# Decay masks of six attention heads: from a DRAM scratch read back by SyncE, to six transfers out of SBUF rows issued by ScalarE

## The chip, the cores and the metric

The kernel runs on one core of a Trainium2 chip. The metric is the device time of one launch, in microseconds. The profile names the engines PE (TensorE; PEld is its weight loads), DVE (VectorE), ACT (ScalarE), POOL (GpSimd) and SP (SyncE). SPq and ACTq are the moments at which SyncE and ScalarE issue a DMA.

## What is computed

Three blocks follow each other: a linear attention with decay, a token-mixing and channel-mixing MLP, and a Fourier mixing with a second MLP. The change lies in the attention, whose reference is:

```python
rel = pos[:, None] - pos[None, :]
Dmask = np.where(rel >= 0, lam[:, None, None] ** rel[None, :, :], 0.0)
for b in range(nb):
    intra = np.einsum('bhic,bhjc->bhij', qb, kb) * Dmask[None]
    intra = np.einsum('bhij,bhjd->bhid', intra, vb)
    inter = np.einsum('bhid,bhde->bhie', qb * lam_pow[None], kv_state)
    out[:, :, sl] = intra + inter
    kv_state = lam_block[None, :, None, None] * kv_state + np.einsum('bhsd,bhse->bhde', kb_dec, vb)
```

There are 2 batches, 8 heads, 768 positions and 64 channels a head, all in float32. Each head has its own decay `lam[h]`, and so its own mask: a triangle of powers of `lam[h]`.

## The kernel before

Heads are taken two at a time: a pair fills the 128 partitions, and there are four pairs in each of two batches. I call them pairs 0 to 3 (first batch) and 4 to 7 (second). The kernel uses blocks of 128 positions, six a sequence. For each pair SyncE loads `kp` (k transposed, 384 KB, L377), q (384 KB, L372) and k with v (768 KB, L373).

`attention_setup` (L299) makes the masks. `pw8` has one row a head: 127 zeros, a one, and the powers of that head's `lam`, doubled seven times on DVE (L317). The mask of a head on 128 partitions is that row read at 128 shifted starts, so that partition p holds elements p to p+127. Heads 0 and 1 are built on DVE by another way (L333 to L350). For heads 2 to 7 the rows go to a DRAM scratch of 8 KB (L320), and `skew` (L324) reads them back as overlapping windows: heads 2 to 5 in one transfer of 256 KB, and heads 6 and 7 in one of 128 KB. All of these are issued by SyncE, among the loads of the pairs. The masks lie in `dT`, a part of the tile `att`.

Each pair then runs three steps. `attention_scores` (L381) multiplies q by k on PE (L393), applies the mask on DVE (L396), and scales q on POOL (L400). `attention_states` (L405) scales k on ACT by a column of the mask (L413), forms the block states on PE (L418) and sums them on DVE (L422, L424). `attention_out` (L428) copies the states on ACT (L435), multiplies on PE (L441, L444) and copies the result on ACT (L446). The words of `EARLY` order these steps: s, u and r with the number of the pair, and `x00` for the first transposes of the MLP (`px`, L461).

In the same stretch the first MLP weights arrive as 64-bit words and are converted to float32: a load (`raw_t`, L190; three of 512 KB come first, one for each tile `w_t1`), an ACT pass (`m_t`, L210), three DVE passes (L235, L236, L238), and a split on ACT (L264) and POOL (L265).

The orders of SP and PE are written out by hand: they are the order of the program. A scheduler orders ACT, DVE and POOL. Every engine takes its own instructions strictly in that order. Each DMA is given one of eight completion counters (DMAHW0 to DMAHW7 in the order below). A DMA that gets a counter that is still in use waits, on the engine that issues it, for the transfer that had it before.

Of the kernel before, what the change touches and what calls it, by code (L numbers as in the profile page):

```python
# [25 lines left out]
P = 128  # L26
C = 128
# [34 lines left out]
def body(ctx: ExitStack, tc: tile.TileContext, qkv, kT, lam, w_tok1, w_tok2,  # L62
         w_ch1, w_ch2, m_ch1, m_ch2, dft, dft_x, out, scratch, singles):
    nc = tc.nc
# [41 lines left out]
    def big_tile(n, dt=F32):  # L106
        return big_p.tile([P, BIG], dt, tag="big", name=n)

    def half_tile(shape, n, dt=F32):
        return half_p.tile(shape, dt, tag="half", name=n)  # L110

    def temp(w, n, dt=F32):
        return t_p.tile([P, 2 * NQ + 2], dt, tag="t", name=n)[:, :w]
# [185 lines left out]
    def attention_setup():  # L299

        pw8 = temp(2 * C, "pw8")[:H]
        nc.sync.dma_start(pw8[:, C:C + 1], lam.rearrange("(h o) -> h o", o=1))
        lam_bc = sm_p.tile([P, H], F32, name="lam_bc")
        nc.scalar.dma_start(lam_bc, lam.rearrange("(o h) -> o h", o=1).broadcast_to([P, H]))
        kp = big_tile("kp").rearrange("p (i s) -> p i s", i=4)[:, :, :S]
        kps = [kp[:, i, :].rearrange("p (c j) -> p c j", j=C) for i in range(4)]
        load_kp(0, 0, kps[0])
        t = half_tile([P, 4, S], "qkv_0_0")
        for i in range(3):
            nc.sync.dma_start(t[:, i, :], qkv[0, 0, :, i])  # L310
        load_kp(0, 1, kps[1])
        nc.vector.memset(pw8[:, 0:C - 1], 0.0)
        nc.vector.memset(pw8[:, C - 1:C], 1.0)
        n = 1
        while n < C:
            w = min(n, C - n)
            ts(out=pw8[:, C + n:C + n + w], in0=pw8[:, C:C + w], scalar1=pw8[:, C + n - 1:C + n], scalar2=None,  # L317
               op0=ALU.mult)
            n *= 2
        nc.sync.dma_start(scratch, pw8)  # L320
        att = big_tile("att")
        dT = att[:, 0:H * C].rearrange("p (h j) -> p h j", h=H)

        def skew(h0, h1):  # L324
            src = bass.AP(scratch.tensor, scratch.offset + h0 * 2 * C, [[1, P], [2 * C, h1 - h0], [1, C]])
            nc.sync.dma_start(dT[:, h0:h1, :], src)

        load_qkv(0, 1)
        skew(2, 6)

        bands = [temp(2 * (C // 2 + C), f"band_{i}").rearrange("p (h j) -> p h j", h=2) for i in range(2)]
        for t_ in bands:
            nc.vector.memset(t_[:, :, 0:C // 2], 0.0)  # L333
        for h in range(2):
            nc.vector.tensor_copy(bands[0][:, h, C // 2:], ident[:, ::-1])
        bd = att[:, (H + NP) * C:(H + NP) * C + 2 * (NC - 1) * P]
        cleared = nc.gpsimd.memset(bd, 0.0).ins
        lp = sm_p.tile([P, 7, 2], F32, name="lp")
        n, i = 1, 0
        while n < C:  # L340
            if n == 1:
                by = lam_bc
            else:
                by = lp[:, i]
                was = lam_bc[:, 0:2] if n == 2 else lp[:, i - 1]
                with tc.issue_after(cleared):
                    nc.gpsimd.tensor_tensor(out=by, in0=was, in1=was, op=ALU.mult)
            for h in range(2):
                src = bands[i % 2][:, h]
                built = stt(out=dT[:, h, :] if 2 * n == C else bands[1 - i % 2][:, h, C // 2:],  # L350
                            in0=src[:, C // 2 - n:C // 2 - n + C], scalar=by[:, h:h + 1], in1=src[:, C // 2:],
                            op0=ALU.mult, op1=ALU.add).ins
            n *= 2
            i += 1
        pw = att[:, H * C:(H + NP) * C].rearrange("p (h j) -> p h j", h=NP)
        bd = bd.rearrange("p (i c j) -> p i c j", i=2, c=NC - 1)

        with tc.issue_after(built):
            for a in range(2):
                nc.vector.tensor_copy(pw[a * D:(a + 1) * D, :, 0:1],  # L360
                                      lam_bc[a * D:(a + 1) * D, a::2].rearrange("p (h o) -> p h o", o=1))
        n = 1
        while n < C:
            nc.gpsimd.tensor_tensor(out=pw[:, :, n:2 * n], in0=pw[:, :, 0:n],
                                    in1=pw[:, :, n - 1:n].to_broadcast([P, NP, n]), op=ALU.mult)
            n *= 2
        pair[0, 0] = t
        return dT, pw, kps, [bd[:, i] for i in range(2)], skew

    def load_qkv(b, hp):  # L370
        t = half_tile([P, 4, S], f"qkv_{b}_{hp}")
        nc.sync.dma_start(t[:, 0, :], qkv[b, hp, :, 0])  # L372
        nc.sync.dma_start(t[:, 1:3, :], qkv[b, hp, :, 1:3])  # L373
        pair[b, hp] = t

    def load_kp(b, hp, kp):
        nc.sync.dma_start(kp, kT[b, hp].rearrange("p (c j) -> p c j", j=C))  # L377
# [74 lines left out]
    h1 = {}  # L452
# [527 lines left out]

    with tc.manual_schedule(engines={ENG.SP, ENG.PE}):
        dT, pw, kps, bds, skew = attention_setup()

        def load(n):
# [174 lines left out]
```

## Time and profile before

| | |
|---|---|
| median of 3 runs | 616.99 us (616.93 to 618.64) |
| the profiled execution | 619.19 us, of which its span is 617.2 us |
| PE busy | 592.4 us (96% of the span) |
| DVE, ACT, POOL busy | 411.1, 269.3, 142.0 us |
| mean granted TensorE clock | 0.994 |

The profile's page cuts the span in 40 slices; a digit is the busy share of a slice in tenths. The windows view gives busy times for any stretch. The timeline lists instructions with what ended the idle time before them: `[2.77 <-DMA raw_t_0d<-w_tok]` says that the engine sat idle for 2.77 us until that transfer had landed.

### The profile page before, as it was taken

Reading aid. Unit: us, or ns where it says so; the run is one execution under the profiler, and the core shown is the slowest. Engines: PE = TensorE matmul, PEld = TensorE weight load, DVE = VectorE, ACT = ScalarE, POOL = GpSimd, SP = SyncE. Lnnn points to the kernel's source line nnn. Section 1 sums busy time; section 2 is a strip of 40 time slices with the busy share of each in tenths; the row PEclk is TensorE's granted clock in tenths of the full one; section 3 lists DMA queues with packets and bytes.
Section 4 is the critical chain, followed back from the end, with each engine's and each line's share of the span. In section 5 each row is a group of like instructions: output and inputs, shape, how many; then the busy total and the mean of one; then the engine's idle time right before and its main releaser. Section 6 shows DMA issues by size and latency. Waiting matters only on the chain. (4 is left out here: it accounts for less than half of the span.)

```text
span 617.2 us, 9594 instructions
## 1 busy us (share of the span) xinstructions
PE 592.4 (96%) x3704; PEld 548.0 (89%) x3704; DVE 411.1 (67%) x768; ACT 269.3 (44%) x536; POOL 142.0 (23%) x119
## 2 busy tenths in 40 slices
PE   8699999999999999999999999999899999999997
PEld 7687899899989998999989999879788887888896
DVE  6697896792656336639696876795697677343435
ACT  2566884653555335244453451333543553211110
POOL 5253333220400220111363210034402232300000
PEclk9899999999999999999999999999999999999999
DMA  7964434333378167100132000002404432000005
GB/s 280 404 240 168 165 134 145 103 115 108 102 255 279 50 192 234 49 1 1 53 88 81 21 1 35 18 1 85 132 5 156 134 121 86 1 1 0 1 1 204
DMA packets 24637, 65.58 MB, mean 106 GB/s; under 512 B 2824, under 2 KB 3984, under 8 KB 24592
## 3 DMA queue, kind: packets, MB, share of 16 engines
q1 hardware_dynamic: 24304, 64.83, 31.4%
q8 instruction: 29, 0.48, 0.4%
q10 hardware_dynamic: 288, 0.14, 0.1%
q14 instruction: 16, 0.13, 0.1%
HBM read 54.99 MB, written 9.97 MB: 105 GB/s over the span
## 5 line engine op out<-in xcount | busy, mean ns | idle before, releaser
L499 DVE SCALAR_TENSOR_TENSOR hid<-ph,hid 128x384 fp32r<-128x384 f32 x68 | 37.7, 554 | 59.3 <-ACT hid L498 59.1
L124 PE MATMUL ac<-w_b,hid 128*128 128x512 f32 x192 | 75.9, 396 | 0.3 <-DVE hid L499 0.3
L123 PE MATMUL ac<-w_b,hid 128*128 128x512 f32 x192 | 75.7, 394 | 0.0
L122 PE MATMUL ac<-w_b,hid 128*128 128x512 f32 x192 | 74.9, 390 | 0.0
L498 ACT ACTIVATE hid<-ph 128x384 fp32r<-128x384 f32 x68 | 33.0, 486 | 80.1 <-PE ph L124 80.1
L122 PE MATMUL ac<-hid,w_b 128*128 128x384 f32 x192 | 65.1, 339 | 1.8 <-ACT hid L498 1.8
L123 PE MATMUL ac<-hid,w_b 128*128 128x384 f32 x192 | 64.9, 338 | 1.3 <-DVE hid L499 1.1
L122 PE MATMUL ph<-uh,w_a 128*128 128x384 f32 x192 | 64.7, 337 | 0.4 <-DVE hid L499 0.4
L124 PE MATMUL ph<-uh,w_a 128*128 128x384 f32 x192 | 64.3, 335 | 0.0
L124 PE MATMUL ac<-hid,w_b 128*128 128x384 f32 x192 | 64.2, 334 | 0.0
L123 PE MATMUL ph<-uh,w_a 128*128 128x384 f32 x192 | 64.2, 334 | 0.0
L265 POOL TENSOR_TENSOR w_a<-m_a,w_a 128x512 fp32r<-128x512 f32 x18 | 25.9, 1437 | 98.1 <-ACT w_a L264 79.9
L124 PEld LDWEIGHTS ac<-w_b,hid 128*128 128x128 f32 x192 | 36.0, 188 | 8.4 <-DVE hid L499 0.8
L123 PEld LDWEIGHTS ac<-w_b,hid 128*128 128x128 f32 x192 | 36.0, 188 | 6.1
L122 PEld LDWEIGHTS ac<-w_b,hid 128*128 128x128 f32 x192 | 36.1, 188 | 5.8
L122 PEld LDWEIGHTS ac<-hid,w_b 128*128 128x128 f32 x192 | 36.1, 188 | 3.4 <-ACT hid L498 3.1
L123 PEld LDWEIGHTS ac<-hid,w_b 128*128 128x128 f32 x192 | 36.1, 188 | 3.0 <-DVE hid L499 2.9
L265 POOL TENSOR_TENSOR w_b<-m_b,w_b 128x512 fp32r<-128x512 f32 x18 | 24.5, 1363 | 61.4 <-ACT w_b L264 37.2
L122 PEld LDWEIGHTS ph<-uh,w_a 128*128 128x128 f32 x192 | 36.1, 188 | 0.9 <-DVE hid L499 0.6
L123 PEld LDWEIGHTS ph<-uh,w_a 128*128 128x128 f32 x192 | 36.1, 188 | 0.1
L124 PEld LDWEIGHTS ph<-uh,w_a 128*128 128x128 f32 x192 | 36.0, 188 | 0.0
L124 PEld LDWEIGHTS ac<-hid,w_b 128*128 128x128 f32 x192 | 36.0, 188 | 0.0
(504 smaller groups left out, 1484.1 us busy)
## 6 DMA issues: line engine op xcount, KB each, us to landing
qkv<-qkv SPq DMA_DIRECT2D x7, 768.0 KB, 7.7
single_scratch<-m_a SPq DMA_DIRECT2D x16, 256.0 KB, 5.0
qkv<-qkv SPq DMA_DIRECT2D x10, 384.0 KB, 5.9
kp<-kT SPq DMA_DIRECT2D x8, 384.0 KB, 6.5
out<-u SPq DMA_DIRECT2D x11, 256.0 KB, 2.1
single_scratch<-m_b SPq DMA_DIRECT2D x10, 256.0 KB, 5.7
raw_t_0d<-w_tok SPq DMA_DIRECT2D x2, 384.0 KB, 7.1
raw_t_1d<-w_tok SPq DMA_DIRECT2D x2, 384.0 KB, 4.5
```

The source lines that it names most:

```text
L122: nc.tensor.matmul(ps, wt[0], xt[0], start=first, stop=False, **kw)
L123: nc.tensor.matmul(ps, wt[0], xt[1], start=False, stop=False, **kw)
L124: nc.tensor.matmul(ps, wt[1], xt[0], start=False, stop=last, **kw)
L265: nc.gpsimd.tensor_tensor(out=t[:, 1, :n], in0=src, in1=f32(t[:, 0, :n]), op=ALU.subtract)
L498: nc.scalar.activation(hi, ps, AF.Relu)
L499: stt(out=lo, in0=ps, scalar=0.0, in1=f32(hi), op0=ALU.max, op1=ALU.subtract)
```

## The change

`skew` no longer goes through DRAM. It issues one transfer a head, from the row of `pw8` in SBUF, and ScalarE issues it. The write of the scratch is gone.

```diff
-        nc.sync.dma_start(scratch, pw8)
         def skew(h0, h1):
-            src = bass.AP(scratch.tensor, scratch.offset + h0 * 2 * C, [[1, P], [2 * C, h1 - h0], [1, C]])
-            nc.sync.dma_start(dT[:, h0:h1, :], src)
+            for h in range(h0, h1):
+                row = pw8[h:h + 1]
+                nc.scalar.dma_start(dT[:, h, :], bass.AP(row.tensor, row.offset, [list(row.ap[0]), [1, P], [1, C]]))
```

The calls `skew(2, 6)` and `skew(6, H)` stay where they are. Each head's transfer moves 128 rows of 512 bytes (64 KB); all 128 are read from one partition, at starts four bytes apart.

On SP, from the load of pair 1's `kp` on, stands before (`qkv_0_1` is pair 1, `qkv_0_2` pair 2, `raw_t1_0d` the first MLP weight):

```order
L377 DMA kp_105<-kT 128x768
L320 DMA pw_scratch<-pw8_101 8x256 [waits DMAHW1_49,DVE_49]
L372 DMA qkv_0_1_123<-qkv 128x768 [waits DMAHW0_49]
L373 DMA qkv_0_1_123<-qkv 128x1536
L326 DMA att_122<-pw_scratch 128x4x128 [waits DMAHW7_49,DMAHW2_49]
L377 DMA kp_105<-kT 128x768 [waits DMAHW3_49]
L372 DMA qkv_0_2_165<-qkv 128x768 [waits DMAHW4_49]
L373 DMA qkv_0_2_165<-qkv 128x1536 [waits DMAHW5_49]
L326 DMA att_122<-pw_scratch 128x2x128 [waits DMAHW6_49]
L377 DMA kp_105<-kT 128x768
L372 DMA qkv_0_3_170<-qkv 128x768 [waits DMAHW0_49]
L373 DMA qkv_0_3_170<-qkv 128x1536 [waits DMAHW1_49]
```

and in the same place on SP with the change:

```order
L377 DMA kp_105<-kT 128x768 [waits DMAHW1_49]
L372 DMA qkv_0_1_122<-qkv 128x768 [waits DMAHW5_49]
L373 DMA qkv_0_1_122<-qkv 128x1536 [waits DMAHW6_49]
L377 DMA kp_105<-kT 128x768 [waits DMAHW7_49]
L372 DMA qkv_0_2_167<-qkv 128x768 [waits DMAHW0_49]
L373 DMA qkv_0_2_167<-qkv 128x1536 [waits DMAHW1_49]
L377 DMA kp_105<-kT 128x768 [waits DMAHW2_49]
L372 DMA qkv_0_3_173<-qkv 128x768 [waits DMAHW3_49]
L373 DMA qkv_0_3_173<-qkv 128x1536 [waits DMAHW4_49]
L190 DMA raw_t1_0d_176<-w_tok1 128x1024 [waits DMAHW5_49]
```

Three issues left SP, and with them the wait for the scratch write. The counters 5, 7, 0, 2, 3 and 4 belong to the masks of heads 2, 3, 4, 5, 6 and 7 just before, so SP's loads of pairs 1 to 3 now wait for masks to land: q of pair 1 for head 2, `kp` of pair 2 for head 3, q of pair 2 for head 4, and `kp`, q and k with v of pair 3 for heads 5, 6 and 7.

On ACT, at the program's start, stands with the change (before, the same rows without the six of L326, and with a wait on DMAHW4 at L413):

```order
L304 DMA lam_bc_103<-lam 128x8
L86 ACT_TABLE_LOAD
L86 ACTIVATE table_89<-table_89 1x1 [waits DVE_49]
L326 DMA att_121<-pw8_101 128x1x128 [waits DMAHW1_49,DVE_49]
L326 DMA att_121<-pw8_101 128x1x128
L326 DMA att_121<-pw8_101 128x1x128 [waits DMAHW0_49]
L326 DMA att_121<-pw8_101 128x1x128 [waits DMAHW2_49]
L326 DMA att_121<-pw8_101 128x1x128 [waits DMAHW3_49]
L326 DMA att_121<-pw8_101 128x1x128 [waits DMAHW4_49]
L413 ACTIVATE qkv_0_0_107<-qkv_0_0_107,att_121 128x5x64 [waits DVE_49] x2
```

The six issues stand ahead of pair 0's product; the last three wait for pair 0's `kp`, q and k to land (counters 2, 3 and 4).

Later on ACT, where the first MLP weights are converted, stands before (`qkv_0_3` is pair 3, `qkv_1_0` pair 4, `m_t1_1` the second weight tile):

```order
L210 ACTIVATE m_t1_0_437<-raw_t1_0d_173 128x512 [waits DMAHW2_49]
L413 ACTIVATE qkv_0_3_170<-qkv_0_3_170,att_122 128x5x64 [waits DMAHW6_49,DMAHW1_49]
L413 ACTIVATE qkv_0_3_170<-qkv_0_3_170,att_122 128x5x64
L210 ACTIVATE m_t1_1_716<-raw_t1_1d_175 128x512 [waits DMAHW3_49]
L210 ACTIVATE m_t1_2_726<-raw_t1_2d_177 128x512 [waits DMAHW4_49]
L413 ACTIVATE qkv_1_0_380<-qkv_1_0_380,att_122 128x5x64 [waits DMAHW7_49]
L413 ACTIVATE qkv_1_0_380<-qkv_1_0_380,att_122 128x5x64
```

and with the change:

```order
L210 ACTIVATE m_t1_0_440<-raw_t1_0d_176 128x512 [waits DMAHW5_49]
L413 ACTIVATE qkv_0_3_173<-qkv_0_3_173,att_121 128x5x64 [waits DMAHW4_49,DMAHW3_49]
L413 ACTIVATE qkv_0_3_173<-qkv_0_3_173,att_121 128x5x64
L413 ACTIVATE qkv_1_0_383<-qkv_1_0_383,att_121 128x5x64 [waits DMAHW2_49]
L413 ACTIVATE qkv_1_0_383<-qkv_1_0_383,att_121 128x5x64
L210 ACTIVATE m_t1_1_719<-raw_t1_1d_178 128x512 [waits DMAHW6_49]
L210 ACTIVATE m_t1_2_729<-raw_t1_2d_180 128x512 [waits DMAHW7_49]
```

The scheduler moved pair 4's product, which waits for pair 4's k and v, ahead of the passes over the second and third weight tiles. The orders of PE and DVE are the same as before. On DVE the product into pair 1's second score tile (L396) also waits for the masks of heads 4 to 7 now, since that tile takes the place of `pw8`, which the six transfers read.

## Rows read from the trace of the kernel before

**Rows 1.** The page's 40 slices: PE, granted clock, DMA.

```profile
PE   8699999999999999999999999999899999999997
PEclk9899999999999999999999999999999999999999
DMA  7964434333378167100132000002404432000005
```

**Rows 2.** Windows: busy us of PE, PEld, DVE, ACT, POOL; clock, DMA share, GB/s.

```profile
4.00:11.00 7.00, 6.93 (x75) 6.04 (x75) 6.31 (x24) 1.01 (x2) 3.46 (x14) 1.00 1.03 416
11.00:15.00 4.00, 3.89 (x68) 3.52 (x66) 1.03 (x4) 1.34 (x4) 2.99 (x2) 1.00 0.80 270
15.00:24.80 9.80, 7.80 (x132) 6.86 (x132) 6.45 (x18) 6.34 (x16) 3.09 (x2) 1.00 1.01 399
24.80:27.90 3.10, 0.00 (x0) 0.00 (x0) 0.43 (x2) 1.16 (x3) 0.00 (x0) 0.84 1.03 407
27.90:34.00 6.10, 6.10 (x64) 5.83 (x64) 6.10 (x13) 2.51 (x5) 1.82 (x1) 0.52 0.95 382
42.00:60.00 18.00, 17.51 (x199) 15.03 (x200) 15.72 (x34) 12.99 (x30) 5.93 (x6) 1.00 0.41 133
```

**Rows 3.** Timeline, first 22 us: `pw8`, and issues on SP (start, us, what).

```profile
0.74 0.38 SPq L302 DMA_DIRECT2D pw<-lam  x1
...
2.17 1.76 DVE L317 TENSOR_SCALAR pw<-pw 8x1 f32<-8x1 f32 x7 [0.83 <-DMA pw<-lam]
3.96 0.30 SPq L320 DMA_DIRECT2D pw_scratch<-pw  x1
...
9.17 0.38 SPq L326 DMA_DIRECT2D att<-pw_scratch  x1
...
13.74 0.51 SPq L373 DMA_DIRECT2D qkv<-qkv  x1
...
21.03 0.33 SPq L373 DMA_DIRECT2D qkv<-qkv  x1
```

**Rows 4.** Waits: SP's own queue, then the first 60 us.

```profile
SPq L326 <- DMA pw_scratch<-pw: 4.0, 1, 4.0
...
DVE st L396 <- DMA att<-pw_scratch: 2.9, 1, 2.9
```

**Rows 5.** DMA issues of the first 40 us: KB each, us to landing.

```profile
att<-pw_scratch SPq DMA_DIRECT2D x1, 256.0 KB, 5.8
att<-pw_scratch SPq DMA_DIRECT2D x1, 128.0 KB, 8.8
```

**Rows 6.** Timeline of ACT.

```profile
7.65 1.01 ACT L413 ACTIVATE qkv<-qkv,att 128x320 f32<-128x320 f32 x2 [5.01 <-DVE att L350]
...
28.21 0.67 ACT L210 ACTIVATE m_t<-raw_t_1d 128x512 f32<-128x512 f32 x1
...
33.14 1.01 ACT L413 ACTIVATE qkv<-qkv,att 128x320 f32<-128x320 f32 x2 [3.17 <-DMA qkv<-qkv]
...
40.18 0.63 ACT L264 ACTIVATE w_t<-m_t 128x512 fp32r<-128x512 f32 x1 [1.37 <-DVE m_t L238]
```

**Rows 7.** Timeline of DVE and POOL, 27 to 41 us.

```profile
27.89 0.69 DVE L236 SCALAR_TENSOR_TENSOR m_t<-raw_t_0d,m_t 128x512 uint32<-128x512 uint32 x1
...
31.29 0.42 DVE L235 TENSOR_SCALAR m_t<-m_t 128x512 uint32<-128x512 uint32 x1
31.62 0.28 DVE L424 SCALAR_TENSOR_TENSOR state<-state,att,u 128x64 f32<-128x64 f32 x1
31.81 1.84 DVE L236 SCALAR_TENSOR_TENSOR m_t<-raw_t_1d,m_t 128x512 uint32<-128x512 uint32 x1
...
38.50 1.65 DVE L238 SCALAR_TENSOR_TENSOR m_t<-raw_t_2d,m_t 128x512 uint32<-128x512 uint32 x1
...
31.28 1.82 POOL L400 TENSOR_TENSOR qkv<-qkv,att 128x640 f32<-128x640 f32 x1 [7.67 <-DMA qkv<-qkv]
```

**Rows 8.** Timeline of PE: the last wait before it runs on.

```profile
41.24 0.65 PE L461 MATMUL px<-ident,xT 128*128 128x128 f32 x4 [0.89 <-ACT xT L446]
```

## The prediction

> **What bounds the kernel now.** I read the page's slices first [rows 1]. PE stands at 9 in nearly every slice, and its clock is full but for the second slice. The change works in the first 30 us or so, so I cut that part into windows [rows 2]. From 4 to 11 us the DMA engines move 416 GB/s at full share; from 11 to 15 only 270 GB/s; then about 400 until 34 us. So loads bound this part. PE pays for it twice: it stands still from 24.80 to 27.90, and then runs at a clock of 0.52 until 34.00. From 42 us on it is busy again without a break worth naming (17.51 of 18 us). What counts, then, is how early PE's last wait ends, at 41.24 [rows 8]. Any shift of that moment goes through to the end, since PE runs its order without slack behind it.
>
> I followed this wait back through the timelines. PE waits for ACT's L446 [rows 8]. ACT stood behind a split of the third weight tile (L264, 40.18) [rows 6], and that waited for DVE's last pass over this tile, 38.50 to 40.15 [rows 7]. DVE was busy in one piece from the second tile's first pass (31.29) to there. ACT's pass that this one needs ran at 28.21 [rows 6]. So weight conversion sets 41.24, not the masks. The masks' own waits are small: SP held 4.0 us for the scratch write, DVE 2.9 us for the mask of pair 1 [rows 4].
>
> **What goes.** SP loses its 4.0 us wait, and the 256 KB and 128 KB that took 5.8 and 8.8 us to land [rows 5]. With them should go the slack stretch from 11 to 15: (416 - 270) x 4 us = 584 KB, or 1.4 us at 416 GB/s. The masks' 393 KB (1 KB = 1000 bytes here) leave SP's queue: at 416 GB/s another 0.9 us.
>
> **What comes: six issues on ACT.** `pw8` is finished at 2.17 + 1.76 = 3.93 us [rows 3]. An issue takes 0.30 to 0.51 us on SP [rows 3], so six take 2 to 3 us. They fall into the 5.01 us in which ACT idles ahead of 7.65 [rows 6]. The last of them waits for pair 0's k, which the product at 7.65 needs anyway. I cost the issuing at nothing; without that cover it would be at most 3 us, once.
>
> **What comes: 768 rows of 512 bytes out of single partitions.** No row of the trace shows a transfer from one partition to all. I bound it. From below: it moves like any load, 393 KB at 416 GB/s = 0.9 us. From above: the one partition is read only as fast as one of the 16 engines moves data, 416 / 16 = 26 GB/s. Then a head takes 65.5 KB / 26 = 2.5 us and six take 15.1 us. The nearest row is the scratch: 16 engines reading overlapping windows of 8 KB. There the rate fell to 270 GB/s at a share of 0.80, and 256 KB needed 5.8 us from issue to landing [rows 2, 5]. A narrow source did cost time, and the new one is a row of 1 KB. So I take the upper pace for the masks. The loads share the same engines: while an engine is held by a mask row it moves no load. The engines won't all be held at once, so I let the loads keep 60% of their pace for 15.1 us: 6.0 us lost. The ends stay 0.9 us and 15.1 us.
>
> [...]
>
> **The sum.** Pair 4's k and v, issued at 21.03 [rows 3], landed at 33.14, where ACT waited 3.17 us for them [rows 6]. With the change: 33.14 - 1.4 - 0.9 + 6.0 = 36.8 us. Now the new order on ACT counts. Pair 4's product (1.01 us) stands ahead of the second tile's pass (0.67 us) [rows 6], so ACT is held until 36.8, and DVE's next pass can start at 36.8 + 1.0 + 0.7 = 38.5 instead of 31.29. Queued behind it on DVE are the sums of pair 3's state, which pair 3's result on PE needs, and the masking of pair 4. From there to the end of the third tile took 40.15 - 31.29 = 8.86 us. One pass in it took 1.84 us where its twin took 0.69, beside a POOL product that started at 31.28 [rows 7]; by 38.5 that product is done, so 1.15 us less: 7.7 us. The end is 38.5 + 7.7 = 46.2, which is 6.0 us after 40.15. PE's last wait moves by as much. The profiled execution took 619.19 us with a span of 617.2; the runs shown have a median of 616.99. I put the shift on the median: 616.99 + 6.0 = **623.0 us**.
>
> Two more waits come with the change, and both lie inside that time. SP's loads wait for masks by way of counters: k and v of pair 3 go out only when head 7 has landed, near 20.5: 4.0 us, 1.4 us for a small transfer to come in (`pw<-lam`, issued at 0.74, let DVE go at 2.17), and 15.1 us. Before they went at 13.74 [rows 3]. And DVE's second score tile of pair 1 waits for all six masks; behind it stands all of DVE, which is ahead of loads that are late anyway.
>
> **Rivals.** *The source costs nothing.* The masks land within 0.9 us of transfer. Then the stream has no slack stretch, and perhaps no straggling either. The bytes up to pair 4's k and v are 9.8 MB (five pairs of 1.57, three weights of 0.52, masks 0.39). At 416 GB/s from 4 us they end near 27.6; they landed at 33.14. If nearly all of that goes, say to 28.3, DVE starts at 30.0, ends 37.7, and PE is 2.5 us earlier: 614.5 us. If only the 1.4 us go, the order on ACT takes it back: 31.7 + 1.7 + 7.7 = 41.1, or 1.0 us later. For it: rows of 512 bytes are what the skews had, too. Against: the narrow source.
>
> *The masks crawl, but the loads run beside them.* Then only the counters bind: pair 3's k and v go at 20.5, and behind them 3.9 MB (those 0.8, three weights 1.6, pair 4 1.6) at 416 GB/s end near 31 us. DVE starts at 32.8, ends at 40.5: 0.35 us later, 617.3 us. For it: ScalarE's queue is a queue of its own. Against: the DMA share is already 1.0 from 4 to 11 us [rows 2], so there is no engine to spare.
>
> **How the numbers follow.** About 0.3% (1.9 us) is what a measurement of this kernel can tell from no change. Forecast, masks slow and holding the loads: 0.50, nearly all slower. Free source: 0.28, of which 0.20 faster and 0.08 the same. Crawling beside the loads: 0.22, with 0.15 the same, 0.03 faster, 0.04 slower. That makes faster 0.23, same 0.25, slower 0.52 (0.02 of the forecast falls within 0.3%). The range reaches down to 614.3, taking in the free source, and up to 628, where the masks take 11 of the 15.1 us from the loads; the full 15.1 would give about 632. Some 0.1 is left out on each side. The slower case alone spans 619.5 to 628.
>
> **What the profile after would show.** If I am right: rows of L326 on ACTq at 4 to 8 us; masks that take over 2 us a head, with heads 6 and 7 landing near 20 us; fewer GB/s between 5 and 20 us than 400; pair 1's scores on PE late; ACT waiting for pair 4's k and v until about 37 us, and DVE's second weight pass right behind it. I am wrong if the stretch from 5 to 15 us stays above 400 GB/s, if head 7 lands before 12 us, or if PE's last wait ends before 42 us.

## The result and the profile after

Measured beside each other, the kernel before took 617.82 us (median of 4 runs, 616.93 to 618.88) and the changed kernel 625.32 us (4 runs, 624.77 to 631.52). The ratio is 1.0138, with a 95% interval of 1.0109 to 1.0167: slower by 6.7 to 10.3 us. The medians alone differ by 7.5 us. The prediction was 623.0 us, slower.

| | before | after |
|---|---|---|
| the profiled execution, its span | 619.19 us, 617.2 us | 624.77 us, 623.0 us |
| pair 4's product starts on ACT (L413) | 33.14 us | 36.94 us |
| second weight tile's first pass on DVE (L235) | 31.29 us | 38.55 us |
| PE's last wait ends (`px`, L461) | 41.24 us | 47.41 us |

The page's slices of PE, granted clock and DMA answer to [rows 1].

```profile
PE   6879999999989999999999999999899999999997
PEclk9799999999999999999999999999999999999999
DMA  7992635135168438200133100002303432000005
```

Only the first slices have changed. The windows that cut them up answer to [rows 2] (start:end, length, busy us of PE, PEld, DVE, ACT, POOL with counts; granted clock, DMA share, GB/s).

```profile
4.00:11.00 7.00, 4.95 (x43) 4.21 (x41) 6.04 (x22) 0.00 (x0) 3.46 (x14) 1.00 0.91 283
11.00:15.00 4.00, 1.21 (x16) 1.05 (x18) 0.00 (x0) 1.01 (x2) 1.42 (x1) 0.77 0.73 81
15.00:20.00 5.00, 3.34 (x26) 2.85 (x24) 1.35 (x5) 1.34 (x4) 0.93 (x1) 0.50 0.94 243
20.00:25.00 5.00, 5.00 (x62) 4.78 (x62) 1.95 (x4) 1.51 (x3) 2.15 (x2) 0.66 1.01 402
...
42.00:49.00 7.00, 4.89 (x70) 4.23 (x72) 6.38 (x14) 4.34 (x11) 4.21 (x4) 1.00 0.65 228
```

Where 416 and 270 GB/s moved before, now 283 and 81 do, and the DMA engines are still counted busy for 0.91 and 0.73 of the time. That pair of numbers is the mark of this change: engines that are counted busy and move little. The records of single packets say with what. The 768 mask rows of 512 bytes run from 7.74 to 20.96 us; a row takes 27 ns at the start, and 144 to 229 ns in the averages of the single microseconds from 11 to 18 us.

The timelines of ACT and SP answer to [rows 3, 6] (start, us, what, idle time before and what ended it).

```profile
3.92 9.21 ACTq L326 DMA_DIRECT2D att<-pw  x6
13.18 1.01 ACT L413 ACTIVATE qkv<-qkv,att 128x320 f32<-128x320 f32 x2 [10.53 <-DMA att<-pw]
...
36.94 1.01 ACT L413 ACTIVATE qkv<-qkv,att 128x320 f32<-128x320 f32 x2 [3.11 <-DMA qkv<-qkv]
...
46.34 0.63 ACT L264 ACTIVATE w_t<-m_t 128x512 fp32r<-128x512 f32 x1 [2.60 <-DVE m_t L238]
```

```profile
10.17 2.92 SPq L373 DMA_DIRECT2D qkv<-qkv  x1
13.14 3.03 SPq L377 DMA_DIRECT2D kp<-kT  x1
16.21 1.96 SPq L372 DMA_DIRECT2D qkv<-qkv  x1
...
21.54 0.33 SPq L373 DMA_DIRECT2D qkv<-qkv  x1
```

Six issues took ACT 9.21 us, and three plain issues of loads held SP for 2 to 3 us each. Ahead of these SP had sent no load since 3.69 us: it waited 6.1 us, until 9.80, for the counter of the first mask. The last row shown of SP is pair 3's k and v, which left at 13.74 before [rows 3]. DVE and PE, answering to [rows 7, 8]:

```profile
38.55 0.43 DVE L235 TENSOR_SCALAR m_t<-m_t 128x512 uint32<-128x512 uint32 x1 [1.20 <-ACT m_t L210]
...
45.62 0.69 DVE L238 SCALAR_TENSOR_TENSOR m_t<-raw_t_2d,m_t 128x512 uint32<-128x512 uint32 x1
```

```profile
47.41 0.66 PE L461 MATMUL px<-ident,xT 128*128 128x128 f32 x4 [1.21 <-ACT xT L446]
```

PE's last wait moved by 6.17 us and the span by 5.8: the shift goes through to the end.

### The profile page after: what moved, and what is told of

Its sections match the earlier page's. It is cut to its first block, busy times and chain, and to the rows that moved or that the text cites. A ratio compares the mean times of both kernels' runs of the same rounds, so it can differ in the third digit from the quotient of the medians.

```text
span 623.0 us, 9594 instructions
## 1 busy us (share of the span) xinstructions
PE 593.1 (95%) x3704; PEld 548.4 (88%) x3704; DVE 413.0 (66%) x768; ACT 269.7 (43%) x536; POOL 141.6 (23%) x119
```

## The experiments

The theory: reading a mask out of one partition is slow, holds the DMA engines, and so delays pair 4's k and v. (The run with four neighbouring source partitions corrects its middle part.) The rivals: the issuing on ACT, the completion counters, and the new order on ACT. Unless it is said otherwise, an edit is shown against the changed kernel. The first four runs share 18 runs of the kernel before (median 617.85 us).

### The same transfers from a wide source

```diff
...
+        wide = sm_p.tile([P, C], F32, name="wide")
+        with tc.issue_after(made):
+            nc.vector.tensor_copy(wide, ident)
...
-                row = pw8[h:h + 1]
-                nc.scalar.dma_start(dT[:, h, :], bass.AP(row.tensor, row.offset, [list(row.ap[0]), [1, P], [1, C]]))
+                nc.scalar.dma_start(dT[:, h, :], wide)
```

> The changed kernel, but each of the six transfers reads one wide tile (128 partitions, 512 bytes from each; a copy of the identity made on VectorE right after the powers) in place of one row of pw8. The masks of heads 2 to 7 are therefore left out (they hold the identity). Number, size, queue and place of the transfers and the new order on ScalarE stay; SyncE's loads still draw the same eight counters. My theory (a source in one partition moves at about 26 GB/s and holds the loads): the six land by 12 us, the stretch from 8 to 20 us is back at 350 GB/s or more, pair 4's k and v land by 32 us instead of 36.9, and the time is 614.5 to 618.5 us. Rival 1 (ScalarE's queue is held by its own issues, or the counters hold SyncE's loads, whatever the source): 622 us or more. Rival 2 (the new order on ScalarE does it): about 623 us.

Measured: 619.6 us, ratio 1.0032 [1.0013, 1.0051]. Windows of 8 to 16 us, and ACT (line numbers are 2 higher here):

```profile
8.00:12.00 4.00, 1.11 (x11) 0.87 (x9) 2.12 (x5) 0.65 (x2) 3.19 (x8) 1.00 1.03 401
...
12.00:16.00 4.00, 3.88 (x32) 3.29 (x34) 1.35 (x5) 1.64 (x5) 2.50 (x3) 0.57 1.07 374
```

```profile
30.45 1.02 ACT L415 ACTIVATE qkv<-qkv,att 128x320 f32<-128x320 f32 x2 [2.04 <-DMA qkv<-qkv]
```

With 128 source partitions every row takes 27 ns, the rate never breaks down, and pair 4's product starts 6.5 us earlier than after, even 2.7 us earlier than before. So most of the loss is the source. Still, the kernel is some 2 us slower than before, and its time lies above the range expected: cheap masks on ACT's queue don't win. Where these 2 us go is not shown. PE's last wait ends at 40.93 here, 0.3 us earlier than before; between 63 and 65 us PE waits twice for ACT's products (0.48 and 0.60 us, before once, 0.42) and is then 0.4 us behind. That is about what the two profiled executions differ by (619.47 and 619.19 us); the rest stands in no trace.

### The old source, issued by ACT

Against the kernel before:

```diff
-        nc.sync.dma_start(scratch, pw8)
+        nc.scalar.dma_start(scratch, pw8)
...
-            nc.sync.dma_start(dT[:, h0:h1, :], src)
+            for h in range(h0, h1):
+                src = bass.AP(scratch.tensor, scratch.offset + h * 2 * C, [[1, P], [1, C]])
+                nc.scalar.dma_start(dT[:, h, :], src)
```

> Half of the change alone: one transfer a head on ScalarE's queue as in the changed kernel, but out of the DRAM scratch as in the kernel before (the scratch is written by ScalarE, too). All masks are right. My theory: without the one-partition source the loads keep their pace, 616 to 620 us (the scratch is a narrow source too, but a faster one). Rival 1 (ScalarE's queue or the counters): as slow as the changed kernel, 623 us or more. Rival 2 (order on ScalarE): 622 us or more as well.

Measured: 621.39 us, ratio 1.0065 [1.0037, 1.0094], above the 616 to 620 us expected. ACT and DVE:

```profile
33.69 1.01 ACT L414 ACTIVATE qkv<-qkv,att 128x320 f32<-128x320 f32 x2 [5.41 <-DMA qkv<-qkv]
34.61 0.64 ACT L210 ACTIVATE m_t<-raw_t_1d 128x512 f32<-128x512 f32 x1
```

```profile
35.28 0.43 DVE L235 TENSOR_SCALAR m_t<-m_t 128x512 uint32<-128x512 uint32 x1 [3.91 <-ACT m_t L210]
```

Pair 4's k and v come at 33.69, nearly as before. But ACT has the order of the changed kernel, L413 (here L414) ahead of L210, so DVE's second pass waits 3.91 us for ACT and starts 4.0 us later than in [rows 7]; PE's last wait ends at 44.15, 2.9 us later. The reordering has a price of its own, with a source that is no narrower. The scratch itself is not slow here: a row takes 27 ns, and 566 rows moved 290 GB/s from 12 to 13 us.

### The narrow source, issued by SP

```diff
-                nc.scalar.dma_start(dT[:, h, :], bass.AP(row.tensor, row.offset, [list(row.ap[0]), [1, P], [1, C]]))
+                nc.sync.dma_start(dT[:, h, :], bass.AP(row.tensor, row.offset, [list(row.ap[0]), [1, P], [1, C]]))
```

> The other half alone: six transfers out of rows of pw8 as in the changed kernel, but issued by SyncE in the places where the two read-backs of the scratch stood. ScalarE issues none of them and keeps the old order around pair 4's product. My theory: the source is what costs, and in SyncE's queue the loads stand strictly behind the masks: 622 to 631 us. Rival 1 (ScalarE held by its issues) and rival 2 (order on ScalarE): near the kernel before, 616 to 619 us.

Measured: 622.47 us, ratio 1.0075 [1.0051, 1.0099]. ACT keeps the order of before; SP's issues and pair 4's product:

```profile
9.43 3.72 SPq L372 DMA_DIRECT2D qkv<-qkv  x1
13.20 3.27 SPq L373 DMA_DIRECT2D qkv<-qkv  x1
```

```profile
35.94 0.56 ACT L413 ACTIVATE qkv<-qkv,att 128x320 f32<-128x320 f32 x1 [3.12 <-DMA qkv<-qkv]
```

On the other queue the masks hold the loads in the same way, and the product is 2.8 us later than before. So the queue isn't the cause. Waits for counters are not needed for it either: SP's longest wait in this stretch is 2.0 us, but single issues take up to 3.72 us. Masks on either queue make the loads late, and with them the product, by 2.8 us from SP's and by 3.8 us from ACT's. With the old order on ACT, narrow masks cost about 4.6 us; the run before put ACT's issuing and order with the old source at 3.5; the changed kernel has both and lost 7.5 in its own comparison.

### The six issues behind pair 0's product

```diff
...
-        skew(2, 6)
...
-        skew(6, H)
...
+        def masks():
+            with tc.issue_after(on_act["prod", 0]):
+                skew(2, H)
...
```

> The changed kernel with the six transfers issued after pair 0's product on ScalarE (near 8.7 us instead of 3.9 us), so that SyncE has sent the loads of pairs 1 and 2 before any mask and only pair 3's loads share counters with masks. My theory in its strong form (the masks hold the engines, some 6 us of load time lost wherever they stand): pair 4's k and v still land at 35 to 38 us and the time is 621 to 626 us. Rival 1 (it is the counters: SyncE's loads of pairs 1 and 2 were not issued because they waited for masks): 616 to 620 us.

Measured: 624.95 us, ratio 1.013 [1.0101, 1.0159], as the changed kernel; pair 4's product starts at 36.72. SP had sent the loads of pairs 1 and 2 by then, so no load of theirs waits for a mask. SP's one long wait, 7.0 us until 14.77, is for the counter of a load, pair 2's q. Windows, and SP (one line number lower for L372 and L377):

```profile
8.00:12.00 4.00, 4.00 (x59) 3.48 (x58) 3.32 (x10) 0.59 (x2) 3.30 (x8) 1.00 1.02 415
12.00:16.00 4.00, 1.26 (x21) 0.90 (x18) 0.74 (x2) 0.00 (x0) 3.08 (x3) 1.00 1.03 355
16.00:20.00 4.00, 2.65 (x25) 2.61 (x27) 1.35 (x3) 2.73 (x7) 0.35 (x1) 0.69 0.70 50
```

```profile
15.15 4.74 SPq L371 DMA_DIRECT2D qkv<-qkv  x1
```

While loads stood in the queues already, the total stayed at 355 GB/s beside the masks. When they were through, SP did not bring up new ones: one issue took 4.74 us, and masks with the little that got in moved 50 GB/s. The counters of masks are not needed for the loss; the hole has only moved.

### ACT's order undone

```diff
...
+        if NP * b + hp == 4:
+            behind = ("abs", 2)
         with tc.issue_after(on_act[behind]):
...
```

Pair 4's L413 is put behind L210 of the third weight tile, and nothing else is moved. This run, the one with half rows and the last two share 24 new runs of before (median 617.45 us).

> The changed kernel with one thing undone: on ScalarE, pair 4's product is held behind the copies of the second and third weight tile, as it stood in the kernel before. The masks' transfers are as in the changed kernel. Theory (the narrow source delays pair 4's k and v, and VectorE's second weight pass waits for ScalarE's copy only because the product with its wait for them stands ahead): pair 4's product still begins at 36.5 to 37.3 us, VectorE's second pass begins near 34 instead of 38.55, and the last wait of TensorE in the attention stage ends 1 to 2 us earlier than 47.41, since pair 4's scores and weights then compete for VectorE; about 1 to 2 us below the changed kernel, some 623.5 to 624.5. Rival (the order on ScalarE is the loss, the transfers are not): back to the kernel before, 617 to 619. Rival (order costs nothing): as the changed kernel, 625.

Measured: 624.71 us, ratio 1.0131 [1.0096, 1.0167]: no gain that can be told from the changed kernel, where 1 to 2 us were expected. The profiled execution was the longest of six (628.28 us), so its times are not compared one by one. It does show two things, on ACT (where L415 and L437 are L413 and L435) and in a window:

```profile
39.27 1.01 ACT L415 ACTIVATE qkv<-qkv,att 128x320 f32<-128x320 f32 x2 [3.14 <-DMA qkv<-qkv]
...
43.15 1.01 ACT L415 ACTIVATE qkv<-qkv,att 128x320 f32<-128x320 f32 x2 [0.93 <-DMA qkv<-qkv]
44.07 0.61 ACT L264 ACTIVATE w_t<-m_t 128x512 fp32r<-128x512 f32 x1
44.59 0.73 ACT L437 ACTIVATE att<-state 64x192 f32<-64x192 f32 x2
```

```profile
42.00:49.00 7.00, 4.86 (x55) 4.41 (x52) 3.29 (x6) 3.98 (x9) 6.65 (x5) 0.62 0.75 283
```

DVE's second pass no longer waits (37.02, ahead of the product). Now ACT waits for pair 4's loads and then for pair 5's (43.15), ahead of the copy of pair 3's state, and PE waits for that. And the clock granted from 42 to 49 us is 0.62, where the changed kernel has 1.00. The late loads hold ACT in another place. What the order alone costs in the changed kernel stays open between nothing and the 3.5 us of the run with the old source.

### Half the bytes, as many rows

```diff
-                nc.scalar.dma_start(dT[:, h, :], bass.AP(row.tensor, row.offset, [list(row.ap[0]), [1, P], [1, C]]))
+                nc.scalar.dma_start(dT[:, h, 0:C // 2], bass.AP(row.tensor, row.offset, [list(row.ap[0]), [1, P], [1, C // 2]]))
...
```

> The changed kernel with the six transfers reading and writing only the left half of each mask: 256-byte rows in place of 512-byte ones, as many rows, the same six issues in the same places; the right halves are left at zero, so the masks of heads 2 to 7 are wrong in this kernel by that and nothing else. Theory (bytes read out of one partition set the pace, near 25 GB/s): the masks' time halves, from some 13 us to 6.5, and pair 4's product begins 3 us earlier, at about 33.9; the whole 3 us shorter than the changed kernel, about 622. Rival (the pace is per row, whatever its length): pair 4's product at 36.9 as before, 625.

Measured: 621.86 us, ratio 1.0074 [1.0047, 1.0101]; the time was put at 622.

```profile
33.17 1.01 ACT L414 ACTIVATE qkv<-qkv,att 128x320 f32<-128x320 f32 x2 [5.00 <-DMA qkv<-qkv]
```

768 rows of 256 bytes run from 7.28 to 14.38 us: 7.1 us in place of 13.2, 28 GB/s against 30. Bytes set the pace, not rows. (The right halves of these masks hold zeros.) Pair 4's product comes 3.8 us earlier.

### Four source partitions: neighbours, 32 apart, 4 apart

The wide source again, cut to four partitions that feed 32 rows each; step 1, 32 or 4 (7 more runs of before, median 618.86 us).

```diff
-                nc.scalar.dma_start(dT[:, h, :], wide)
+                rows = wide[0:4:1]
+                nc.scalar.dma_start(dT[:, h, :], bass.AP(rows.tensor, rows.offset, [list(rows.ap[0]), [0, 32], [1, C]]))
```

> The wide-source kernel (six transfers of 64 KB from an identity tile, the masks of heads 2 to 7 left out) with the source narrowed to partitions 0, 1, 2 and 3: each of the four feeds 32 rows of 512 bytes of every transfer; queue, order, sizes and destination as in the changed kernel. If a single partition is what is slow, four of them carry four times as much: mask bytes near 100 GB/s, six transfers over in some 4 to 5 us, pair 4's product begins at 31 to 32.5 us (30.45 with 128 source partitions, 36.94 with one). If neighbouring partitions share one way out, the pace is that of one partition, 20 to 28 GB/s, pair 4's product at 36 to 38, the whole at 624 to 626. [...]

> As the run before it, with source partitions 0, 32, 64 and 96. If the count of partitions sets the pace, as in that run with four partitions free of each other: pair 4's product at 31 to 32.5. If they leave by shared ways, something between: mask bytes near 50 GB/s with two ways, about 8 us for the six, pair 4's product near 33 to 34, the whole some 2.5 to 4 us below the changed kernel, 621 to 622.5. [...]

> As the two before it, with source partitions 0, 4, 8 and 12. If the count of partitions sets the pace, it equals the other two. If ways are shared by neighbouring groups of four, these are four ways: mask bytes near 100 GB/s, 4 to 5 us for the six, pair 4's product at 31 to 32.5, the whole at 619.5 to 621.5. [...]

| source partitions | pair 4's product | median | ratio to before |
|---|---|---|---|
| 0, 1, 2, 3 | 37.73 us | 625.99 us | 1.0121 [1.0106, 1.0137] |
| 0, 32, 64, 96 | 34.84 us | 622.69 us | 1.0066 [1.0051, 1.0081] |
| 0, 4, 8, 12 | 34.71 us | 623.93 us | 1.0089 [1.0063, 1.0116] |

Windows (length, granted clock, DMA share, GB/s): first the changed kernel, in the microsecond from 11 and in the three from 9 us, then the neighbours, all with masks alone on the way; last the source 32 apart, with 12 GB/s of loads beside the masks. The row of the source 4 apart reads the same, with 18 GB/s of loads.

```profile
11.00:12.00 1.00, 1.00 0.68 27
9.00:12.00 3.00, 1.00 0.68 43
```

```profile
16.00:17.00 1.00, 0.50 0.16 25
```

```profile
13.00:14.00 1.00, 0.50 0.30 81
```

One partition: 27 GB/s at a share of 0.68. Four neighbours: 25 GB/s at a share of 0.16. Far fewer engines are held, and the pace is the same, so it is set on the side of the source, and the four neighbours together are read no faster than the one partition. These 25 to 27 GB/s are the steady pace: the neighbours' rows moved 25 to 26 GB/s in each microsecond from 14 to 18 us, the changed kernel's 20 to 28 from 11 to 18. Short stretches ran above it (43 GB/s from 9 to 12 us, 44 from 13 to 14 with the neighbours); no run explains them.

The neighbours also correct the theory. From 16 to 17 us the engines are counted busy for 0.16, and still no load moves, and pair 4's product comes later than with one partition. SP stood in long issues:

```profile
13.56 3.55 SPq L376 DMA_DIRECT2D qkv<-qkv  x1
17.16 2.82 SPq L380 DMA_DIRECT2D kp<-kT  x1
```

So the loads can be late with most of the engines free, and held engines are not the whole cause. What this run shares with the changed kernel, with the run on SP's queue and with the late one is a slow source beside which single issues of loads stretch to between 2.8 and 4.74 us; with the source 32 apart, where SP waits for counters of masks as well, no issue of a load takes more than 0.71 us after the first masks. What makes an issue long, no trace shows.

With the source spread, mask rows alone make up 62 to 69 GB/s, and the product is 3 us earlier. The step of 32 came out slightly slower than expected (34.84 us against 33 to 34, and 622.69 against 621 to 622.5). The third expectation missed: with ways out that groups of four share, step 4 was to be faster than step 32, and their products are 0.13 us apart. In the microsecond from 13 us 122 to 134 rows took 31 to 32 ns each, which is some four engines at work all the time, so the reason may be that four partitions keep only four engines busy. The trace doesn't name the engines; this is argued, not shown, and the two and the four ways out that the expectations count with are the author's assumption: no run tells them apart.

### Masks without any transfer

From the kernel before: TensorE makes the powers, VectorE multiplies them with a triangle of ones, and ScalarE prepares the rows while it is idle.

```diff
...
-        nc.sync.dma_start(scratch, pw8)
...
+        for h in range(2, H):
+            nc.scalar.activation(rows[(h - 2) // 3][:, (h - 2) % 3 * C:((h - 2) % 3 + 1) * C], pw8[:, C - 1:2 * C - 1], AF.Copy, scale=by[:, h:h + 1])
...
+                nc.tensor.matmul(ps, pw8[:, C - 1:2 * C - 1], rows[i],
+                                 start=True, stop=True)
+                tt(out=dT[:, 2 + 3 * i:5 + 3 * i, :], in0=ps.rearrange("p (h j) -> p h j", h=3),
+                   in1=tri.rearrange("p (o j) -> p o j", o=1).to_broadcast([P, 3, C]), op=ALU.mult)
...
```

> The kernel before with no mask transfer at all: TensorE makes the powers of heads 2 to 7 in two matrix products of eight rows behind pair 0's scores, VectorE multiplies them with a triangle of ones. The scratch write, its wait on SyncE and the two reads are gone, and nothing is put on ScalarE's queue but six short scalings in its idle time. Theory (the dip and the mask bytes in SyncE's queue cost 2 to 3 us of loading, and pair 4's k and v set the chain): the loads run at about 400 GB/s from 4 to 36 us, pair 4's k and v land at 30 to 31 instead of 33.1, and TensorE's last wait of the stage ends at 39 to 41 instead of 41.24; 615 to 617.5. Rival (VectorE's work between 31 and 40 us binds then, as in the run with the wide source): 617 to 619.

> As the run before it, and in addition VectorE sums pair 3's states ahead of the second weight tile's passes, and ScalarE copies pair 3's last result ahead of the third weight tile. If VectorE's order is what binds once the loads are early, TensorE's last wait of the stage ends at 37 to 38.5, 613 to 615.5. If the loads behind (weights and pairs 5 to 7) bind in its place, the gain is given back between 45 and 60 us and the time is that of the run before.

```profile
8.00:12.00 4.00, 4.00 (x45) 2.82 (x43) 3.96 (x13) 1.01 (x2) 2.26 (x8) 1.00 1.02 414
12.00:16.00 4.00, 4.00 (x64) 3.71 (x64) 3.23 (x10) 2.73 (x7) 4.00 (x3) 1.00 1.03 409
```

```profile
28.86 1.01 ACT L427 ACTIVATE qkv<-qkv,att 128x320 f32<-128x320 f32 x2 [2.94 <-DMA qkv<-qkv]
```

The first of the two: 615.91 us, ratio 0.9981 [0.9961, 1.0002]. The dip from 11 to 15 us is gone, pair 4's product is 4.3 us earlier than before (more than the 2 to 3 us expected), and the time only 1.5 us shorter, not separable from none. The second also moves VectorE's and ScalarE's order: 615.88 us, ratio 0.9976 [0.9959, 0.9993], with

```profile
38.69 0.66 PE L478 MATMUL px<-ident,xT 128*128 128x128 f32 x4 [1.15 <-ACT xT L463]
...
50.36 0.50 PE L123 MATMUL h<-x,w_t 128*128 128x512 f32 x1 [1.02 <-DVE x L118]
```

PE's wait ends 2.6 us earlier than before, and its next one, for DVE, 2.0 us earlier (50.36, before 52.38). The medians keep 1.6 us of that. It is the one version here whose interval lies below the kernel before, by a quarter of a per cent, and it can't be told from the first of the two (615.88 and 615.91 us). That is the time of the second outcome expected, but not by its path: near 60 us PE is still 1.3 us ahead of the first (59.28 against 60.55 at the same group of L418).

## Why the prediction held, point by point

- **Masks at the pace of one engine (15.1 us): right, somewhat long.** 13.2 us, 30 GB/s on average. The reason given, that one partition is read no faster than one engine moves data, got the number, but no engine is the limit: rows kept the engines busy to 0.68, about eleven of 16. The runs with four neighbours and half rows put the limit at the source (25 GB/s at a share of 0.16; 28 GB/s with rows of half the bytes). The nearest row named, the scratch, was no support: its rows take 27 ns, 290 GB/s in the run with the scratch on ACT's queue. The dip from 11 to 15 us before comes after a stretch in which SP sent nothing (5.1 to 9.17 us); what made it, no run separates. So the choice of the upper pace was in part luck.
- **Loads keep 60% for 15.1 us, 6.0 us lost: mis-sized, and two errors cancelled.** From 7.74 to 20.96 us the loads moved 1.99 MB, 36% of 416 GB/s: 8.4 us lost. That an engine held by a mask row moves no load fits the trace while the engines are nearly full: from 16 to 19 us mask rows held a share of 0.43 and the rest 0.54, 0.97 together, and the rest moved 221 GB/s, about 410 to a full share; from 4 to 7.74 us, without masks, it was 403 GB/s at 1.02. In all, the 32.9 us up to pair 4's product (from 4 us on, masks counted) fall 3.3 MB short of 416 GB/s, which is 7.9 us. Before, the windows of [rows 2], the last of them cut at 33.14 us (below), fall 0.8 MB short, or 2.0 us. The loss grew by 5.9 us, where the sum had 6.0 - 1.4 - 0.9 = 3.7. What made up for it was not in the sum: when pair 4's k and v had landed, 11.3 MB had moved before, 1.5 MB more than the 9.8 MB up to that load; after, 10.4 MB, only 0.6 MB more. Less of the later loads ran beside it, 0.9 MB or 2.1 us. 5.9 - 2.1 = 3.8: predicted 36.8, measured 36.94. That the two errors are of like size is luck.

```profile
27.90:33.14 5.24, 5.24 (x57) 5.07 (x59) 5.24 (x11) 1.66 (x3) 1.82 (x1) 0.50 1.02 407
```

- **Issuing costs nothing: mis-sized.** 9.21 us in place of 2 to 3, and pair 0's product started at 13.18, not 7.65. It cost nothing that shows at the end: pair 1's loads came later than that in any case, and the run with the late issues, where pair 0's product runs at 7.58, takes as long. The cover named (ACT's 5.01 us of idle time) did not suffice; another one, the late loads, hid the rest. With the wide source the six took 7.30 us as well, though each issue took only some 0.5 us: the rest are waits for counters.
- **ACT's order, DVE at 38.5, 7.7 us of chain, 46.2: right within 0.1 us** (38.55 to 46.31). It is the path that this kernel took; with the order undone another one was as long, so the order is not shown to be needed. One pass took 1.84 us here too, beside another product, so the 1.15 us taken out of the chain came off elsewhere, above all in the third tile's last pass: 0.69 us in place of 1.65 [rows 7].
- **PE's wait + 6.0: right, 6.17.** The step that was off lies behind it: the shift was put on a median of 616.99. The profiled execution before, 619.19 us, lies above the medians of before in all of these comparisons (617.45 to 618.86), and the one after, 624.77, is the shortest of its four. Profile to profile the change costs 5.6 us, median to median 7.5. Of the 2.3 us that the prediction fell short, 0.8 us lie in the median of before (617.82 in place of 616.99) and 1.5 us in the shift.
- **Rivals.** *Free source*: the wide source shows what it would have given. Of its two results, 2.5 us faster and 1.0 us slower by ACT's order, the second was near in the number: 619.6 against 617.85. Its mechanism is not what that run shows, since PE's last wait ends earlier there, not 1.0 us later. *Masks crawl beside the loads, only counters bind* (617.3): refuted, since the loads kept 36% beside the masks, and the run on SP's queue is late without a long wait for a counter. ACT's queue is a row of its own on the page (q10, 0.53 MB after, 0.14 before), but the time of its packets counts on the same 16 engines.

## What to carry to other kernels

A transfer that reads all its rows out of one SBUF partition, or out of four neighbours, moves some 25 to 30 GB/s here, and while it does so, the loads come late (pair 4's product by 2.8 to 4.6 us): look in the windows for few GB/s, whatever the DMA share (0.68 and 0.16 here), and in the timelines for long issues. Moving it to another queue does not make it fast (4.6 us lost with the masks on SP's queue, 7.5 on ACT's), spreading its source does (62 to 69 GB/s from four partitions 4 or 32 apart, 27 ns a row from 128), and this small table was cheaper computed than copied, by a quarter of a per cent. Where a scheduler orders an engine, look which instruction with a wait now stands ahead of which without: with the old source, that and the issuing cost 3.5 us here.

## What the runs showed beyond that

- An issue is not a fixed cost. Beside slow rows the same instruction that takes 0.33 us took 1.96 to 4.74 us on SP, and 0.55 to 3.33 us on ACT. Why, the trace has no row for.
- With 27 GB/s on the way, the profile counts the DMA engines busy to 0.68, since a row of 27 ns becomes one of some 200 ns. The DMA share says that engines are counted busy, not that they move anything.
- PE lost clock as well: from 15 to 20 us of the kernel after the granted clock was 0.50, behind a stretch (11 to 15 us) in which PE was busy for 1.21 of 4 us. Not every such stretch is followed by this: with half rows PE was busy for 1.12 us from 12 to 16 us, and the clock was 1.00 from 16 to 20.
